# Three attention units take their decay rows from TensorE instead of from DRAM, and the loads of the opening are put in another order

## The chip, the cores and the metric

The kernel runs on one core of a Trainium2 chip. The metric is the device time of one execution in microseconds (us). Times are given as a median over runs; one further execution was recorded by the profiler, and every duration below is from that one.

## The reference

`reference()` chains two blocks. The first is an mLSTM over q, k, v of shape batch 4 x heads 8 x 768 steps x 40, with one input gate, one forget gate and 40 output gates per step:

```python
m_new  = np.maximum(f_gate[:, :, t] + m, i_gate[:, :, t])
f_stab = np.exp(f_gate[:, :, t] + m - m_new)
i_stab = np.exp(i_gate[:, :, t] - m_new)
C = f_stab * C + i_stab * (v_t outer k_t)
n = f_stab * n + i_stab * k_t
y[:, :, t] = sigmoid(o_gate_t) * (C @ q_t) / max(|n . q_t|, 1)
```

The second is `silu(x @ w_in) @ w_out` on the 3072 rows of 320 that result (w_in is 320 x 2048, w_out 2048 x 320). The weights reach the kernel as 64-bit words and are decoded on the chip.

## The kernel before, in words

**Units.** The 768 steps are cut into 6 chunks of 128. A chunk of one batch, with its 8 heads, is a *unit*; there are 24, unit n being chunk n // 4 of batch n % 4. Within a chunk the recurrence is written as attention with a decay matrix: `Dm[s, h, t] = exp(LF[h, t] + a[s, h])` where t >= s, and 0 elsewhere. `LF` is the running sum of the stabilised log forget gates of the chunk, `a` (kept transposed as `aT`) holds the input-gate part. A unit loads `raw` (q and k, two DMAs in `load_qk`), `kvo` (k, v, output gate in one tile, `load_kvo`), `D` (the rows of LF, each spread over all 128 partitions, `load_d`) and, from chunk 1 on, `qt` and `lq` (`load_q`). It then computes `decay` (mask on GpSimd at L355, exponentials on ScalarE at L365, and `fd`, the decay over the whole chunk), `misc` (tanh of the output gate at L370), `scores` (q.k products at L394; VectorE makes `vw` at L406 and multiplies the scores into `D` at L413), `values` (products at L433, then x on VectorE), `state` (products `pu` at L462) and `xpose` (transposition of x, rounded into `xh` with its remainder `xl`).

**Gates.** `gates(lo, hi)` works on 32 rows (batch x head) by hi - lo steps on VectorE: a running maximum `m_t`, elementwise steps, the sums `LF`, the input part `i_t`; a TensorE transposition turns `i_t` into `aT`. `LF` is then written to a DRAM tensor `LFd`, and every unit's `D` is read back from there with a broadcast. Before the change this is done for chunk 0 first and later for chunks 1 to 5.

**Steps.** Three units form a step (8 steps): 384 rows go through the MLP in 16 column blocks fc. `mm1(fc)` makes 8 products into the PSUM tile `ph` (L532); ScalarE and VectorE form the activation `g` (step 0) or its two parts `gh`, `gl`; `mm2(fc)` adds the products with the second weights into three `pout` tiles (L572), two fc later. Step 0 uses the unrounded `wo` (one product per row block), later steps the rounded `woh` with its remainder `wol`.

**Weights.** 18 parts are loaded by `wload` into the ring of ten "big" buffers (`wrc`, `wri` for w_in, `wro` for w_out) and decoded by `wmake`: one ScalarE instruction (L184), four VectorE instructions (L185, L186, L189, L195), then for w_in a rounding on ScalarE (L205, L215) and a remainder on VectorE (L206, L216). The decoding runs beside the first units and step 0.

**Order.** SyncE (SP) issues nearly all DMAs, strictly in program order. The five pieces of later units are mixed into the steps' loop by the table SCHED through `piece(i)`, where unit n's first piece also issues all loads of unit n + 2. The order on TensorE, ScalarE, VectorE and GpSimd is set by the tile scheduler when the program is built; the function `gates` stands in a block that fixes VectorE's order by hand.

The loads of the opening stand in the program like this before the change:

```python
wload(1); units[0].load_qk(); gates(0, L)
units[0].load_kvo(); units[0].load_d(); prepare(0)
units[1].load_qk(); units[1].load_d(); units[1].load_kvo(); wload(1)
units[2].load_qk(); units[2].load_d(); units[2].load_kvo()
units[0].scores(); prepare(1); gates(L, S); wload(2)
```

Of the kernel before, what the change touches and what calls it, by code (L numbers as in the profile page):

```python
# [8 lines left out]
F32 = mybir.dt.float32  # L9
# [8 lines left out]
L = 128  # L18
# [5 lines left out]
UPS = 3  # L24
# [20 lines left out]
def mlstm_mlp_kernel(  # L45
# [35 lines left out]
    woh = cp.tile([128, NFC, DM], F32R, name="woh")  # L81
# [3 lines left out]
    wo, wol = {}, {}  # L85
# [3 lines left out]
    f_t, i_t, m_t, LF = (  # L89
        pb.tile([BH, S], F32, tag="big", name=n) for n in ("f_t", "i_t", "m_t", "LF")  # L90
    )
# [7 lines left out]
    nc.sync.dma_start(bm, bmask)  # L99
    nc.gpsimd.memset(one, 1.0)  # L100

    def gates(lo, hi):
# [22 lines left out]
        nc.sync.dma_start(LFd[:, 0:H, lo:hi], LF[:, lo:hi])  # L125
        nc.scalar.dma_start(LFd[:, H, lo:hi], LF[0:B, lo:hi])
# [93 lines left out]
    def split_out(i):  # L220

        full, hi = wo.pop(i), woh[:, 2 * i : 2 * i + 2, :]
# [46 lines left out]
    class Unit:  # L269
# [5 lines left out]
        def load_d(self):  # L275
            n, c, b = self.n, self.c, self.b
            sl = slice(c * L, (c + 1) * L)
            self.Dm = p3.tile([128, H, L], F32, tag="D", name=f"D{n}")
            nc.sync.dma_start(
                self.Dm, LFd[b, 0:H, sl].unsqueeze(0).broadcast_to([128, H, L])  # L280
            )
# [38 lines left out]
        def load(self):  # L320
            self.load_d()
            self.load_qk()
            self.load_kvo()
            self.load_q()

# [21 lines left out]
        def decay(self, hf):  # L347

            b, c = self.b, self.c
            if hf == 0 and c < NC - 1:  # L350
                self.fd = p3.tile([KS, H], F32, tag="fd", name=f"fd{self.n}")
                nc.scalar.activation(self.fd, self.Dm[:KS, :, L - 1], AF.Exp)  # L352
            d = self.Dm[:, hf * HH : (hf + 1) * HH, :]
            r = b * H + hf * HH
            nc.gpsimd.affine_select(  # L355
                out=d,
                in_=d,
                compare_op=ALU.is_ge,
                fill=NEG,
                base=0,  # L360
                pattern=[[0, HH], [1, L]],
                channel_multiplier=-1,
            )
            for h in range(HH):
                nc.scalar.activation(  # L365
                    d[:, h, :], d[:, h, :], AF.Exp, bias=aT[:, c, r + h : r + h + 1]
                )

# [138 lines left out]
    class Step:  # L507
# [48 lines left out]
        def mm2(self, fc):  # L556
# [7 lines left out]
            if j == 0:  # L564
                ops = [(gh, wo[fc // 2][:, fc % 2, :])]
            else:
                hi, lo = woh[:, fc, :], wol[fc // 2][:, fc % 2, :]
                ops = [(gh, hi), (gh, lo), (gl, hi)]
# [48 lines left out]
    def piece(i):  # L617

        n, k = divmod(i, 5)
        u = units[n]  # L620
        if k == 0:
            if n + 2 < NU:
                units[n + 2].load()
            u.scores()
        elif k == 2:
            u.values()
        elif k == 3:
            u.state()
# [17 lines left out]
    wload(1)  # L646
    units[2].load_qk()
# [124 lines left out]
```

## Time and profile before

| | us |
|---|---|
| runs | 515.27, 519.13, 521.06; median 519.13 |
| the profiled execution: its own time | 516.28 |
| its span | 514.5 |
| TensorE (PE) busy | 483.6 (94% of the span) |
| VectorE (DVE) busy | 335.0 (65%) |
| ScalarE (ACT) busy | 267.2 (52%) |
| GpSimd (POOL) busy | 95.6 (19%) |

The profiled execution took 1.8 us more than its span; the rest lies around the program. A share is an average over the whole span: TensorE's 94% is made of a long stretch without gaps and an opening in which it often stands still. The profile's rows give a start, a duration, the engine, the line, the operation with output and inputs, and in brackets the idle time ahead and what ended it. An fp32 product is recorded as two rows, so "x8" at L394 is four products.

### The profile page before, as it was taken

What the parts mean: (1) busy time and instruction counts of PE and PEld (TensorE: products, weight loads), DVE (VectorE), ACT (ScalarE), POOL (GpSimd) and SP (SyncE); (2) the same over time, 40 slices, a digit from 0 to 9 for tenths busy, and PEclk for the clock granted to TensorE, in tenths of its full rate; (3) what the DMA queues carried; (4) which work ended last, traced back from release to release, by engine and by line L of the source; (5) the groups of instructions that cost most, each with busy time, mean ns of one, the idle gap of its engine ahead of it and who ended that gap; (6) DMA issues with size and microseconds to landing.
All of it is one profiled execution on the core that took longest, in us unless ns stands there. A gap on an engine that the chain in (4) does not pass through costs nothing.

```text
span 514.5 us, 8611 instructions
## 1 busy us (share of the span) xinstructions
PE 483.6 (94%) x3098; PEld 463.4 (90%) x3098; DVE 335.0 (65%) x687; ACT 267.2 (52%) x647; POOL 95.6 (19%) x139
## 2 busy tenths in 40 slices
PE   1498899999999999999999999999899999999996
PEld 1397888888899998999899999999899999999996
DVE  6499999953796677667756597546665654444332
ACT  1556767431775467447664557526664433334332
POOL 0211305321233212313221222112210000000000
PEclk9999999999999999999999999999999999999999
DMA  3999996153476437543560367333660000001001
GB/s 100 301 351 242 256 324 199 33 155 108 129 173 172 122 86 215 156 137 109 183 167 33 108 180 203 105 106 102 189 170 31 29 27 14 0 1 40 0 3 38
DMA packets 52525, 65.54 MB, mean 127 GB/s; under 512 B 3195, under 2 KB 40479, under 8 KB 52483
## 3 DMA queue, kind: packets, MB, share of 16 engines
q1 hardware_dynamic: 48963, 60.95, 42.2%
q10 hardware_dynamic: 3520, 4.04, 2.3%
q8 instruction: 24, 0.39, 0.3%
q14 instruction: 18, 0.15, 0.1%
HBM read 60.94 MB, written 4.04 MB: 126 GB/s over the span
## 4 chain that ended last, share of the span: by engine, by line
PE 68%; DMA 16%; ACT 7%; DVE 4%; issue 2%; SPq 1%; POOL 1%; POOLq 0%; ACTq 0%; DVEq 0%
PE ph L532 28%; PE pout L572 28%; DMA D<-LFd 8%; DMA raw<-in_qk_dram 7%; PE po L433 5%; ACT D L365 3%; PE ps L394 3%; PE po L424 2%; ACT st L338 1%; PE pu L462 1%; PE px L495 1%; DMA lq<-LFd 1%; POOL D L355 1%; DMA wrc<-in_w_in_dram 1%; DVE st L340 1%
## 5 line engine op out<-in xcount | busy, mean ns | idle before, releaser
L532 PE MATMUL ph<-xh,wh 128*128 128x384 f32 x384 | 135.8, 354 | 2.4 <-DVE g L540 1.7
L532 PE MATMUL ph<-xl,wh 128*128 128x384 f32 x384 | 130.2, 339 | 0.0
L545 DVE SCALAR_TENSOR_TENSOR th<-th,ph 128x384 f32<-128x384 f32 x112 | 61.4, 549 | 79.5 <-ACT th L536 79.5
L572 PE MATMUL pout<-woh,gh 128*128 128x320 f32 x336 | 106.9, 322 | 2.1 <-ACT gh L550 2.0
L572 PE MATMUL pout<-wol,gh 128*128 128x320 f32 x336 | 102.8, 308 | 0.0
L551 DVE TENSOR_TENSOR gl<-th,gh 128x384 fp32r<-128x384 f32 x112 | 68.7, 614 | 48.9 <-ACT gh L550 46.6
L536 ACT ACTIVATE th<-ph 128x384 f32<-128x384 f32 x128 | 62.1, 485 | 70.3 <-PE ph L532 63.3
L572 PE MATMUL pout<-woh,gl 128*128 128x320 f32 x336 | 97.9, 312 | 0.6 <-DVE gl L551 0.5
L532 PE MATMUL ph<-xh,wl 128*128 128x384 f32 x256 | 86.9, 339 | 0.0
L550 ACT CAST gh<-th 128x384 fp32r<-128x384 f32 x112 | 56.8, 510 | 48.4 <-DVE th L545 47.1
L532 PEld LDWEIGHTS ph<-xh,wh 128*128 128x128 f32 x384 | 72.8, 190 | 4.7 <-DVE g L540 2.0
L532 PEld LDWEIGHTS ph<-xl,wh 128*128 128x128 f32 x384 | 72.7, 189 | 1.0
L365 ACT ACTIVATE D<-D,aT 128x128 f32<-128x128 f32 x192 | 59.7, 390 | 15.2 <-POOL D L355 15.0
L572 PEld LDWEIGHTS pout<-woh,gh 128*128 128x128 f32 x336 | 63.1, 188 | 3.9 <-ACT gh L550 3.0
L572 PEld LDWEIGHTS pout<-wol,gh 128*128 128x128 f32 x336 | 63.3, 188 | 0.0
L572 PEld LDWEIGHTS pout<-woh,gl 128*128 128x128 f32 x336 | 61.2, 188 | 1.4 <-DVE gl L551 1.2
L433 PEld LDWEIGHTS po<-kvo,D 128*128 128x128 f32 x384 | 54.3, 215 | 1.3 <-ACT wti L184 0.8
L433 PE MATMUL po<-kvo,D 128*128 128x41 f32 x384 | 54.7, 297 | 0.4 <-issue 0.4
L340 DVE TENSOR_TENSOR st<-raw,st 40x512 fp32r<-40x512 f32 x64 | 45.0, 703 | 6.7 <-ACT st L338 5.4
L532 PEld LDWEIGHTS ph<-xh,wl 128*128 128x128 f32 x256 | 48.4, 189 | 0.0
L355 POOL TENSOR_SCALAR_AFFINE_SELECT D<-D 128x512 f32<-128x512 f32 x48 | 32.8, 706 | 77.3 <-ACT fd L352 61.5
L338 ACT CAST st<-raw 120x512 fp32r<-120x512 f32 x64 | 35.9, 621 | 16.1 <-DMA raw<-in_qk_dram 16.1
(77 smaller groups left out, 546.3 us busy)
## 6 DMA issues: line engine op xcount, KB each, us to landing
raw<-in_qk_dram SPq DMA_DIRECT2D x32, 480.0 KB
D<-LFd SPq DMA_DIRECT2D x24, 512.0 KB
kvo<-in_kvo_dram SPq DMA_DIRECT2D x24, 484.0 KB
wro<-in_w_out_dram SPq DMA_DIRECT2D x8, 640.0 KB
wri<-in_w_in_dram SPq DMA_DIRECT2D x8, 512.0 KB
out_dram<-ob ACTq DMA_DIRECT2D x24, 160.0 KB
qt<-in_qp_dram SPq DMA_DIRECT2D x20, 180.0 KB
lq<-LFd SPq DMA_DIRECT2D x60, 60.0 KB
```

The source lines that it names most:

```text
L338: nc.scalar.copy(t, raw)
L340: nc.vector.tensor_tensor(out=t[r0 : r0 + D, :], in0=raw[r0 : r0 + D, :], in1=t[r0 : r0 + D, :].bitcast(F32), op=ALU.subtract,)
L355: nc.gpsimd.affine_select(out=d, in_=d, compare_op=ALU.is_ge, fill=NEG, base=0, pattern=[[0, HH], [1, L]], channel_multiplier=-1,)
L365: nc.scalar.activation(d[:, h, :], d[:, h, :], AF.Exp, bias=aT[:, c, r + h : r + h + 1])
L394: nc.tensor.matmul(ps[:, j, :], k_[:, cs], q_[:, cs], start=True, stop=True)
L433: nc.tensor.matmul(po[:, h, :], self.Dm[:, h, :], self.vt[:, h, :], start=first, stop=(h == H - 1))
L532: nc.tensor.matmul(ph, w, x, start=(i == 0), stop=(i == len(ops) - 1))
L536: nc.scalar.activation(th, ph, AF.Tanh, scale=0.5)
L545: nc.vector.scalar_tensor_tensor(out=th, in0=th, scalar=1.0, in1=ph, op0=ALU.add, op1=ALU.mult)
L550: nc.scalar.copy(gh, th)
L551: nc.vector.tensor_tensor(out=gl, in0=th, in1=gh.bitcast(F32), op=ALU.subtract)
L572: nc.tensor.matmul(self.po[t], g[:, ts], w, start=(fc == 0 and i == 0), stop=(last and i == len(ops) - 1),)
```

## The change

- **Decay rows of units 0, 1, 2 by products.** `load_d` of these units allocates `D` and issues no DMA. `decay` makes, per half of the heads, four products of a column of the identity, broadcast to 128 columns, with `LF` of the chunk (32 rows by 128): each spreads one row of LF over 128 partitions of a PSUM tile `pd`. The exponentials read `pd` and write `D`; the mask follows them, with fill 0 in place of -1e30 ahead of them. The `pd` tiles of units 0 and 1 take buffers of `psO` (three), those of unit 2 buffers of `psH` (two). `fd` is no longer made in chunk 0, where nothing reads it.
- **Gates in one tile.** `f_t`, `i_t`, `m_t`, `LF` are slices of one tile `G` in a pool of one buffer whose next tenant is `woh`; four "big" buffers are thereby free from the start. `gates(0, L)` and `gates(L, S)` stand one behind the other at the beginning; `LF` is written to `LFd` once, for all chunks, by `gates_out` from SP's queue.
- **Loads.** The order of the opening is new (below). In the loop, the loads of unit n + 2 are issued with three pieces of unit n: `kvo` and `D` with the first, `raw` with the second, `qt` and `lq` with the fourth.

```diff
+    pg = pool("pg", 1)
+    G = pg.tile([BH, 4, S], F32, tag="g", name="G")
+    f_t, i_t, m_t, LF = (G[:, i, :] for i in range(4))
...
+    def gates_out():
+        nc.sync.dma_start(LFd[:, 0:H, :], LF)
+        nc.sync.dma_start(LFd[:, H, :], LF[0:B, :])
...
-        nc.sync.dma_start(LFd[:, 0:H, lo:hi], LF[:, lo:hi])
-        nc.scalar.dma_start(LFd[:, H, lo:hi], LF[0:B, lo:hi])
...
+            if n < UPS:
+                return
             nc.sync.dma_start(
                 self.Dm, LFd[b, 0:H, sl].unsqueeze(0).broadcast_to([128, H, L])
...
+            if n < UPS:
+                to, tag = (psH, "h") if n == UPS - 1 else (psO, "o")
+                e = to.tile([128, HH, L], F32, tag=tag, name=f"pd{n}_{hf}")
+                for h in range(HH):
+                    nc.tensor.matmul(
+                        e[:, h, :],
+                        ident[:BH, r + h : r + h + 1].broadcast_to([BH, 128]),
+                        LF[:, c * L : (c + 1) * L],
...
             if n + 2 < NU:
-                units[n + 2].load()
+                units[n + 2].load_kvo()
+                units[n + 2].load_d()
             u.scores()
+        elif k == 1:
+            if n + 2 < NU:
+                units[n + 2].load_qk()
...
-    wload(1)
-    units[0].load_qk()
     with tc.manual_schedule(engines={mybir.EngineType.DVE}):
         gates(0, L)
+        gates(L, S)
+    units[0].load_qk()
+    wload(1)
...
     units[2].load_kvo()
+    gates_out()
+    wload(3)
     units[0].scores()
     prepare(1)
-    gates(L, S)
-    wload(2)
```

**SP's queue, the opening.** `LFd` is the DRAM copy of the gate sums, `D` a unit's decay rows, `wrc`, `wri`, `wro` the weight parts. Before:

```order
L97 DMA f_t<-in_fg_dram 32x768
L99 DMA bm<-in_bmask_dram 120x123
L171 DMA wrc_110<-in_w_in_dram 64x1024
L172 DMA wrc_110<-in_w_in_dram 64x1024
L291 DMA raw_113<-in_qk_dram 40x1024 x2
L125 DMA LFd<-LF 4x8x128
L302 DMA kvo_132<-in_kvo_dram 128x968
L279 DMA D_134<-LFd 128x8x128
L291 DMA raw_153<-in_qk_dram 40x1024 x2
L279 DMA D_156<-LFd 128x8x128
L302 DMA kvo_158<-in_kvo_dram 128x968
```

After the change, from `wrc` on (ahead of it stand only `G<-in_fg_dram` and unit 0's two `raw`):

```order
L172 DMA wrc_143<-in_w_in_dram 64x1024
L173 DMA wrc_143<-in_w_in_dram 64x1024
L307 DMA kvo_146<-in_kvo_dram 128x968
L296 DMA raw_170<-in_qk_dram 40x1024 x2
L307 DMA kvo_174<-in_kvo_dram 128x968
L168 DMA wri_176<-in_w_in_dram 128x2x512
L675 DMA bm<-in_bmask_dram 120x123
L296 DMA raw_179<-in_qk_dram 40x1024 x2
L307 DMA kvo_183<-in_kvo_dram 128x968
L102 DMA LFd<-G 4x8x768
L103 DMA LFd<-G 4x768
L168 DMA wro_187<-in_w_out_dram 128x2x640
```

The write of the gate sums, which the loads of kvo and everything later stood behind, has moved behind the loads of all three units; the weights `wro` now stand behind it, and no row reads `D` for the first three units.

**ScalarE and VectorE, units 0 and 1 after the change.** The first fence is ScalarE from the decoding of the first weight part (L185) on; L389 is the tanh of a unit's output gate, L382 the exponentials.

```order
L185 ACT_TABLE_LOAD
L185 ACTIVATE wtc_259<-wrc_143 128x512
L389 ACTIVATE kvo_146<-kvo_146 128x320
L216 CAST wh<-wtc_259 64x512 x2
L389 ACTIVATE kvo_174<-kvo_174 128x320
L382 ACTIVATE D_148<-pd_0_149,aT 128x128 x4
L382 ACTIVATE D_148<-pd_1_159,aT 128x128 x4
```

The second is VectorE up to unit 0's scores (L432); ahead of its first row stand unit 0's `vw` and the five sums L125 of the later chunks. The G rows are gates of chunks 1 to 5, the wti and wto rows weight decoding, `vw_238` is unit 1's.

```order
L128 TENSOR_TENSOR G<-G 32x640
L186 TENSOR_SCALAR wti_345<-wti_345 128x512
L131 TENSOR_TENSOR G<-G 32x640
L187 TENSOR_SCALAR wti_345<-wti_345 128x512
L190 SCALAR_TENSOR_TENSOR wti_345<-wri_176,wti_345 128x512
L140 COPY aT<-pt_132 128x160
L196 SCALAR_TENSOR_TENSOR wti_345<-wri_176,wti_345 128x512
L425 TENSOR_TENSOR vw_238<-kvo_174,D_173 128x328
L207 TENSOR_TENSOR wl<-wti_345,wh 128x2x256
L186 TENSOR_SCALAR wto_391<-wto_391 128x640
L187 TENSOR_SCALAR wto_391<-wto_391 128x640
L432 TENSOR_TENSOR D_148<-ps_0_193,D_148 128x512
```

Before, the gates' rows stood ahead of every row of unit 0, and the two rows of unit 0's scores followed its `vw` directly; now gates of the later chunks, a part of `w_in` and the first half of the first part of `w_out` stand between them.

**TensorE, the first products of the MLP.** Before, unit 3's values (`po_549`) and state (`pu_591`) stand in the first `ph`:

```order
L433 MATMUL po_549<-kvo_397,D_392 128x41 x4
L532 MATMUL ph_0_459<-xh_284,wh 128x384
L462 MATMUL pu_591<-vw_514,kvo_397 120x123 x2
L462 MATMUL pu_591<-vw_514,kvo_397 80x82
L433 MATMUL po_549<-kvo_397,D_392 128x41 x4
L532 MATMUL ph_0_459<-xl_285,wh 128x384
```

After it, the products of `ph_0` and `ph_1` follow unit 2's transposition directly; the last of `ph_1` (of the products of unit 3, `ps_0_501` and `ps_1_502` are the scores) and what comes then:

```order
L551 MATMUL ph_1_527<-xh_292,wl 128x384
L551 MATMUL ph_1_527<-xh_292,wh 128x384
L551 MATMUL ph_1_527<-xl_293,wh 128x384
L413 MATMUL ps_0_501<-raw_402 128x128 x4
L413 MATMUL ps_1_502<-raw_402 128x128 x4
L551 MATMUL ph_2_566<-xh_292,wh 128x384
```

Unit 3's scores (`ps_0_501`, `ps_1_502`), its values and its state, which stood ahead of the MLP's first products or among them, have moved behind `ph_1` and further.

More of the change, by code (lines that the diff above doesn't have):

```diff
@@ L80, in mlstm_mlp_kernel @@
     wl = cp.tile([128, 2, DFF], F32R, name="wl")
-    woh = cp.tile([128, NFC, DM], F32R, name="woh")
     pq = pool("pq", DFF // 256)
-    wo, wol = {}, {}
+    wo, wol, woh = {}, {}, {}
+    pg = pool("pg", 1)
     BH = B * H
-    f_t, i_t, m_t, LF = (
-        pb.tile([BH, S], F32, tag="big", name=n) for n in ("f_t", "i_t", "m_t", "LF")
-    )
+    G = pg.tile([BH, 4, S], F32, tag="g", name="G")
+    f_t, i_t, m_t, LF = (G[:, i, :] for i in range(4))
     one = cp.tile([BH, 1], F32, name="one")
@@ L98, in mlstm_mlp_kernel @@
     nc.scalar.dma_start(i_t, ig)
-    nc.sync.dma_start(bm, bmask)
     nc.gpsimd.memset(one, 1.0)
+    def gates_out():
+        nc.sync.dma_start(LFd[:, 0:H, :], LF)
+        nc.sync.dma_start(LFd[:, H, :], LF[0:B, :])
     def gates(lo, hi):
@@ L220, in split_out @@
     def split_out(i):
-        full, hi = wo.pop(i), woh[:, 2 * i : 2 * i + 2, :]
+        if not woh:
+            woh[0] = pg.tile([128, NFC, DM], F32R, tag="g", name="woh")
+        full, hi = wo.pop(i), woh[0][:, 2 * i : 2 * i + 2, :]
         to, tag = (pq, "wo") if i else (pw, "wt")
@@ L318, in load_q @@
                     )
[L320 to L324, printed above, removed]
         def split(self, hf, which):
@@ L347, in decay, with mask @@
         def decay(self, hf):
-            b, c = self.b, self.c
-            if hf == 0 and c < NC - 1:
-                self.fd = p3.tile([KS, H], F32, tag="fd", name=f"fd{self.n}")
+            n, b, c = self.n, self.b, self.c
+            if hf == 0 and 0 < c < NC - 1:
+                self.fd = p3.tile([KS, H], F32, tag="fd", name=f"fd{n}")
                 nc.scalar.activation(self.fd, self.Dm[:KS, :, L - 1], AF.Exp)
-            d = self.Dm[:, hf * HH : (hf + 1) * HH, :]
+            d = e = self.Dm[:, hf * HH : (hf + 1) * HH, :]
             r = b * H + hf * HH
[L355 to L363, printed above, removed]
+            if n < UPS:
[6 more added lines that the diff above has]
+                        LF[:, c * L : (c + 1) * L],
+                        start=True,
+                        stop=True,
+                    )
+            def mask(fill):
+                nc.gpsimd.affine_select(
+                    out=d,
+                    in_=d,
+                    compare_op=ALU.is_ge,
+                    fill=fill,
+                    base=0,
+                    pattern=[[0, HH], [1, L]],
+                    channel_multiplier=-1,
+                )
+            if n >= UPS:
+                mask(NEG)
             for h in range(HH):
                 nc.scalar.activation(
-                    d[:, h, :], d[:, h, :], AF.Exp, bias=aT[:, c, r + h : r + h + 1]
+                    d[:, h, :], e[:, h, :], AF.Exp, bias=aT[:, c, r + h : r + h + 1]
                 )
+            if n < UPS:
+                mask(0.0)
         def misc(self):
@@ L566, in mm2 @@
             else:
-                hi, lo = woh[:, fc, :], wol[fc // 2][:, fc % 2, :]
+                hi, lo = woh[0][:, fc, :], wol[fc // 2][:, fc % 2, :]
                 ops = [(gh, hi), (gh, lo), (gl, hi)]
@@ L627, in piece @@
         elif k == 3:
+            if n + 2 < NU:
+                units[n + 2].load_q()
             u.state()
@@ L646, in mlstm_mlp_kernel @@
     wload(1)
+    nc.sync.dma_start(bm, bmask)
     units[2].load_qk()
```

## The prediction

> **What bounds the kernel now.** I read the page's head first, then the windows of each stage, then TensorE's rows in the opening.
>
> ```profile
> span 514.5 us, 8611 instructions
> 5.00:10.00 5.00, 0.00 (x0) 0.00 (x0) 4.07 (x10) 1.94 (x2) 0.00 (x0) 1.00 0.27 79
> 15.00:20.00 5.00, 1.13 (x7) 1.03 (x8) 1.41 (x3) 1.56 (x5) 1.21 (x2) 1.00 1.03 277
> 30.00:40.00 10.00, 10.00 (x54) 9.06 (x53) 8.86 (x22) 5.95 (x14) 0.40 (x1) 1.00 1.04 322
> 40.00:50.00 10.00, 8.61 (x39) 6.95 (x40) 10.00 (x27) 6.72 (x17) 1.67 (x2) 1.00 1.03 247
> 80.00:100.00 20.00, 20.00 (x109) 16.69 (x108) 20.00 (x37) 12.85 (x34) 7.60 (x9) 1.00 0.45 133
> 150.00:200.00 50.00, 50.00 (x347) 49.42 (x347) 36.26 (x74) 30.27 (x79) 13.91 (x21) 1.00 0.52 141
> ```
>
> In a window's row stand its length, then the busy time of TensorE, its weight loads, VectorE, ScalarE and GpSimd, then the clock, the share of the DMA engines and GB/s. From 80 us on TensorE hardly stands still (20.00 of 20, 50.00 of 50): loads there are hidden, and the end moves by what the dense stretch's beginning moves. The opening is another matter. At 5 to 10 us the DMA engines are used to 0.27, since SP's queue stands before the write of the gate sums; from 15 us on they are full. The chain of waits shows what TensorE waited for then:
>
> ```profile
> 2.27 4.22 DMA wrc<-in_w_in_dram
> 19.38 8.59 DMA D<-LFd
> ```
>
> The second row is unit 2's decay rows, 8.59 us from issue to landing. So the change attacks something real: a round trip through DRAM, and 3 x 512 KB of reads. TensorE's rows (start, duration, ..., in brackets the idle time ahead) show what the opening is made of:
>
> ```profile
> 11.47 2.08 PE L394 MATMUL ps<-raw 40*128 40x128 f32 x16
> 23.27 2.07 PE L394 MATMUL ps<-raw 40*128 40x128 f32 x8 [1.73 <-DVE D L413]
> 25.27 1.93 PE L433 MATMUL po<-kvo,D 128*128 128x41 f32 x8
> 41.87 1.42 PE L462 MATMUL pu<-vw,kvo 128*120 128x123 f32 x6 [0.21 <-DVE x L447]
> 44.47 0.69 PE L495 MATMUL px<-ident,x 128*128 128x128 f32 x2 [1.18 <-DVE x L450]
> 45.92 3.09 PE L394 MATMUL ps<-raw 40*128 40x128 f32 x16
> 48.94 0.69 PE L495 MATMUL px<-ident,x 128*128 128x128 f32 x2
> 50.89 1.90 PE L433 MATMUL po<-kvo,D 128*128 128x41 f32 x8 [0.43 <-issue]
> 52.59 0.67 PE L532 MATMUL ph<-xh,wh 128*128 128x384 f32 x1
> 53.06 1.29 PE L462 MATMUL pu<-vw,kvo 128*120 128x123 f32 x6
> 55.79 0.67 PE L532 MATMUL ph<-xl,wh 128*128 128x384 f32 x1
> 56.26 0.52 PE L532 MATMUL ph<-xh,wl 128*128 128x384 f32 x1
> 56.58 0.52 PE L532 MATMUL ph<-xh,wh 128*128 128x384 f32 x1
> 58.60 0.33 PE L532 MATMUL ph<-xh,wl 128*128 128x384 f32 x1
> 58.78 0.33 PE L532 MATMUL ph<-xh,wh 128*128 128x384 f32 x1
> 61.46 0.44 PE L532 MATMUL ph<-xh,wh 128*128 128x384 f32 x1 [1.65 <-DVE g L540]
> ```
>
> Three readings. Unit 0's values begin at 25.27, held by its decay. From there to the first MLP products at 55.79 the engine stands still for only 0.21 + 1.18 + 0.43 = 1.8 us: this stretch is work, not waiting. And that work runs at half speed: at 56.26 and 56.58 the products start 0.32 us apart, at 58.60 and 58.78 0.18. The page prints a clock of 1.00 throughout, so the spacing is what to trust.
>
> **The change part by part.** I follow the new program from its start to its first values product.
>
> ```profile
> 6.57 1.28 ACT L184 ACT_TABLE_LOAD   x1 [6.57 <-DMA wrc<-in_w_in_dram]
> 14.07 1.26 ACT L215 CAST wh<-wtc 64x512 fp32r<-64x512 f32 x2 [5.55 <-DVE wtc L195]
> 19.45 2.44 ACT L365 ACTIVATE D<-D,aT 128x128 f32<-128x128 f32 x8 [0.74 <-POOL D L355]
> 22.79 0.47 ACT L370 ACTIVATE kvo<-kvo 128x320 f32<-128x320 f32 x1 [0.78 <-DMA kvo<-in_kvo_dram]
> 18.79 1.22 POOL L355 TENSOR_SCALAR_AFFINE_SELECT D<-D 128x512 f32<-128x512 f32 x2 [17.48 <-ACT fd L352]
> 8.55 0.43 DVE L185 TENSOR_SCALAR wtc<-wtc 128x512 f32<-128x512 f32 x1 [0.93 <-ACT wtc L184]
> 11.09 0.67 DVE L189 SCALAR_TENSOR_TENSOR wtc<-wrc,wtc 128x512 uint32<-128x512 uint32 x1
> 11.69 1.67 DVE L122 TENSOR_TENSOR_SCAN LF<-one,f_t 32x128 f32<-32x128 f32 x5
> 13.97 0.81 DVE L130 TENSOR_TENSOR i_t<-i_t,LF 32x640 f32<-32x640 f32 x1
> 14.92 0.71 PE L136 MATMUL pt<-ident,i_t 32*128 32x32 f32 x5 [1.37 <-DVE i_t L130]
> 14.20 1.94 SPq L302 DMA_DIRECT2D kvo<-in_kvo_dram  x1
> 22.05 0.63 SPq L125 DMA_DIRECT2D LFd<-LF  x1
> ```
>
> *The products.* 24 of them are added. The trace has none of this kind; the nearest rows are scores products with 40 rows, 0.52 us each where they stand alone (four in 2.07, at 23.27) and 0.26 where two share the time (eight in 2.08, at 11.47). The new ones all use the same 32 rows, so 0.52: 12.4 us, from about 5.5 (the gates begin at 3.6) to about 18. At the lower price they would end near 12. Neither end costs anything: the exponentials that read the last of them stand behind 20 others on ScalarE and come at 19 or later, and TensorE had nothing else to do then. If that cover went, the price is what sticks out, at most 1 us.
>
> *ScalarE's order.* It loads its table only when `wrc` has landed, at 6.57 before. Unit 0's `raw`, 320 KB, now goes ahead of it and `bm`, 58 KB, behind: 262 KB, 0.9 us at 277 GB/s, 2.2 at the 121 GB/s that the row of 4.22 us gives for 512 KB. I take 1.3: 7.9. Table 1.28 and the first decoding 0.66: 9.8. VectorE's four decoding rows, two of each kind, 2.2: 12.0. The two casts 1.26: 13.3. Unit 1's tanh 0.47: 13.8. Only then eight exponentials, 2.44: 16.2, and the second mask, half of 1.22: 16.8. That tanh waits for unit 1's kvo, up to which the queue holds 2.3 MB; at 277 GB/s, from 2.3 us on, it lands near 11. It costs nothing up to 13.3, and one for one from there.
>
> *VectorE's order.* `vw` 0.5: 17.3. The five sums 1.67: 19.0, and LF is whole. Two gate rows of 0.81 and a decoding row of 0.43: 21.0. Transpositions 0.71, then unit 0's scores 2.08 and the first half of unit 1's 2.04: 25.8 on TensorE. Meanwhile SP writes the sums (two issues, 1.4) and issues the first `wro` at 20.4. In an all but empty queue 512 KB took 4.22, so 4.3: 24.7. Two ScalarE and VectorE steps on it, 0.8 and 1.0, stand ahead of unit 0's scores: 26.4. The row itself 0.65 frees the bank for the other half of unit 1's scores, 2.05. **Unit 0's values begin at 29.1, 3.8 us later than at 25.27.** The wait for D has become a wait for the weights.
>
> *From there to the MLP.* Before, 25.27 to 55.79 is 30.5 us. Out of it go the 1.8 of idle time, unit 3's scores (45.92 to 48.94: 3.0) and its values and state with one product of `ph` (50.89 to 55.79: 4.9), which now stand behind `ph_1`. That leaves 20.8: `ph_0` begins at 49.9 and not at 55.8.
>
> *What was put off.* It comes back at full speed:
>
> ```profile
> 92.96 1.08 PE ps L394 x8
> ```
>
> Eight records, four products, in 1.08: unit 3's scores 2.2. For its values and state I halve the 4.4 of before: 2.2. The sixteen products of `ph_0` and `ph_1` take 4.0 of 55.79 to 59.8 for fifteen, so 4.3. The change of speed came 2.5 us after the dense products began; they now begin at another moment, and every further microsecond at half speed costs about 0.45, so 0 to 1.5, taken as 0.8. The idle 1.65 ahead of 61.46 goes, since unit 3's scores now lie there; if VectorE is late all the same, it stays. Sum: 49.9 + 4.3 + 0.8 + 2.2 + 2.2 = 59.4, against 61.46 for the same work: **2.1 us earlier**, 0.4 if the gap stays. Behind this point the loop's new load order matters only if TensorE waits there. The longest row of its waits from 62 us on is
>
> ```profile
> PE pout L572 <- ACT gh L550: 2.0, 3, 1.2
> ```
>
> 2.0 us in three waits, none of the list for a DMA. I count nothing, plus or minus 1 us; the cover is TensorE's own work, and a load that came late would cost one for one.
>
> The profiled execution took 516.28, which gives 514.2. It lies near the fast end of the runs; their median of 519.13 gives 517.0. Part of that spread may be the opening's transfers, which half leave the path, so I set 516.
>
> **A rule against the trace.** In the window of 30 to 40 us TensorE is busy 10.00 of 10 and yet at half speed. The Trainium skill ("TensorE: Matmul & The Clock Gate", "Part 1: The HAM clock gate") says that the clock doubles after one busy window of some 3.4 us. By that rule the 12 us of new products would lift it at once, and the idle time behind them, from 18 to 21, is too short for it to fall: that is the first rival, and its 510 to 511. The trace disagrees as far as records show busy time: they filled 10 us without a rise. Products with few rows or columns may not count as busy; no run here shows it.
>
> **The rivals.**
>
> *The engine goes fast early.* The new products are a longer unbroken run than any ahead of 29.98 before. If they lift the clock and it holds, the 20.8 us to the MLP shrink towards 11. VectorE then binds: it is full in 40 to 50 (10.00 of 10) and would hold `ph_0` near 46, 4 us earlier than in the sum; with 1 to 2 us in `ph_0` and `ph_1` that is 5 to 6 more, 510 to 511. Against it: the long run at 30 to 40 lifted nothing, and the scores at 45.92, 40 rows like the new products' 32, neither.
>
> *VectorE holds step 0.* It is full from 40 to 100 (20.00 of 20 in 80 to 100) with weight decoding, which the change leaves as it is. If TensorE overtakes it, the gain is eaten and the time is 518 to 519. For it: that full stretch, and the 1.65 us wait. Against it: only that one wait.
>
> *The weights come late (slower).* Unit 0's scores stand behind `wro` on VectorE, and `wro` behind the gate sums on SP. In the full queue unit 1's kvo took from 14.20 to 22.79, 8.6 us. Had `wro` that, everything from 25.8 on would move 4.3 later: 521 or so, and with unit 1's tanh held as long, 524. It decides from a landing at 26.8 on, where the 2.1 are gone. For it: three engines wait in a row there. Against it: the queue should be empty by 18.
>
> That the round trip stays is ruled out for units 0 to 2: SP's rows have no read of D for them.
>
> **How the numbers follow.** Forecast 0.50 (513 to 519); fast early 0.18 (508 to 513); VectorE 0.15 (518 to 520); late weights 0.17 (520 to 525). A measurement here tells about 1%, 5.2 us: under 514 faster, over 524.3 slower. Faster: the second case and a third of the first, 0.35. Slower: half of the fourth and a little, 0.10. The rest, 0.55, is within. The range 508 to 523 leaves out the two far ends.
>
> **What would show it.** Right: no D rows before unit 3's; values from 28 to 30; `ph_0` at 49 to 51, spacing 0.32 and then 0.18 within 6 us; no `g` wait ahead of `ph_2`. Wrong: 0.18 spacing or scores of 0.27 each before 45; `wro` landing after 27; TensorE waiting for `wh` or `wo` in 60 to 100; or new waits behind 110, where the loop's load order would show.

## The result, and the profile after

The changed kernel takes 514.4 us (median of 20 runs, 508.8 to 518.4) beside 516.7 for the kernel before in the same session: a ratio of 0.9937, 95% interval 0.9908 to 0.9965. A repetition gave 514.4 beside 515.6, ratio 0.9969, with an interval (0.9932 to 1.0006) that touches 1. Medians are over all runs, ratios over the fast runs alone (runs more than 1.5% above a kernel's fastest are left out), so a ratio can differ a little from the quotient of the medians. The size of the forecast, 516.0 and 2 to 3 us less than before, was right. Its origin, as the experiments show, was not.

The profiled execution of the changed kernel took 516.9 us. It contains 10.2 us at half clock behind 138 and 213 us, which the execution shown of before does not have, so only its opening is compared directly.

The page's head and the windows (columns as in the prediction) of the changed kernel:

```profile
span 515.2 us, 8685 instructions
5.00:10.00 5.00, 4.38 (x20) 4.41 (x21) 0.87 (x3) 1.75 (x2) 0.00 (x0) 1.00 1.03 266
15.00:20.00 5.00, 2.07 (x8) 1.77 (x8) 4.90 (x7) 5.00 (x20) 3.17 (x4) 1.00 0.21 70
30.00:40.00 10.00, 10.00 (x54) 9.40 (x54) 10.00 (x23) 3.33 (x5) 1.02 (x1) 1.00 0.59 206
100.00:150.00 50.00, 47.81 (x283) 42.40 (x282) 35.08 (x67) 22.08 (x55) 14.20 (x19) 0.93 0.45 125
```

The DMA engines now work from 5 us on (1.03 where it was 0.27) and have little to do from 15 to 20 (0.21 where it was 1.03), since the three reads of decay rows are gone and the other loads that ran then before now come earlier. From 5 to 10 TensorE has the new products. The last row shows the half clock as a mean of 0.93 over the window.

TensorE's rows in the opening of the changed kernel (start, duration, engine, line, operation, count, idle time ahead in brackets):

```profile
5.62 4.60 PE L360 MATMUL pd<-G,ident 32*128 32x128 f32 x20 [5.62 <-DVE G L125]
10.09 4.61 PE L360 MATMUL pd<-G,ident 32*128 32x128 f32 x20
15.43 2.07 PE L360 MATMUL pd<-G,ident 32*128 32x128 f32 x8 [0.73 <-ACT D L382]
23.82 0.74 PE L137 MATMUL pt<-ident,G 32*128 32x32 f32 x5 [6.31 <-DVE G L131]
24.49 3.78 PE L413 MATMUL ps<-raw 40*128 40x128 f32 x24
28.90 2.07 PE L413 MATMUL ps<-raw 40*128 40x128 f32 x8 [0.63 <-DVE D L432]
30.90 1.93 PE L452 MATMUL po<-kvo,D 128*128 128x41 f32 x8
51.86 0.69 PE L551 MATMUL ph<-xh,wh 128*128 128x384 f32 x1 [0.57 <-ACT xh L521]
55.82 0.49 PE L551 MATMUL ph<-xh,wh 128*128 128x384 f32 x1
56.14 0.35 PE L551 MATMUL ph<-xl,wh 128*128 128x384 f32 x1
56.95 1.71 PE L413 MATMUL ps<-raw 40*128 40x128 f32 x16
58.59 0.44 PE L551 MATMUL ph<-xh,wh 128*128 128x384 f32 x1
```

The 48 records of the 24 products end at 17.5, and 6.31 us of idle time follow. Unit 0's values begin at 30.90, 5.6 us later than before, and the first MLP product stands at 51.86, 3.9 us earlier than the 55.79 at which before's dense products began. Products are 0.32 us apart up to 56.14 and 0.18 to 0.19 from there. Unit 3's scores stand behind the two product groups, 1.71 us where they cost 3.09 before. Nothing waits ahead of `ph_2`. Its start at 58.59 and unit 3's values and state, 2.30 (61.72 to 64.02), make 60.9 for the work that before had behind it at 61.46: 0.6 us gained, not 2.1.

Why the values are later than forecast stands on VectorE and GpSimd in the same stretch:

```profile
15.45 0.63 POOL L369 TENSOR_SCALAR_AFFINE_SELECT D<-D 128x512 f32<-128x512 f32 x1 [14.07 <-ACT D L382]
20.48 2.28 POOL L369 TENSOR_SCALAR_AFFINE_SELECT D<-D 128x512 f32<-128x512 f32 x2 [0.54 <-ACT D L382]
15.58 1.17 DVE L114 TENSOR_TENSOR G<-G 32x640 f32<-32x640 f32 x1
16.79 1.14 DVE L117 TENSOR_TENSOR G<-G 32x640 f32<-32x640 f32 x1
19.10 2.05 DVE L125 TENSOR_TENSOR_SCAN G<-one,G 32x128 f32<-32x128 f32 x5
21.08 1.18 DVE L128 TENSOR_TENSOR G<-G 32x640 f32<-32x640 f32 x1
22.19 0.84 DVE L186 TENSOR_SCALAR wti<-wti 128x512 f32<-128x512 f32 x1
```

Gate rows of 32x640 took 1.14 to 1.18 beside the masks and 0.81 in the trace of before; the five sums 2.05 for 1.67; a decoding row 0.84 for 0.43. The decay masks of the first units, which now follow the exponentials, fall upon VectorE's gate rows. In the chain, the two transfers of the sum came nearly as forecast:

```profile
2.59 5.57 DMA wrc<-in_w_in_dram
22.44 3.93 DMA wro<-in_w_out_dram
```

### The profile page after: what moved, and what is told of

Same layout as the page of the kernel before. It is cut to its first block, busy times and chain, and to the rows that moved or that the text cites. A ratio compares the mean times of both kernels' runs of the same rounds, so it can differ in the third digit from the quotient of the medians.

```text
span 515.2 us, 8685 instructions
## 1 busy us (share of the span) xinstructions
PE 493.1 (96%) x3146; PEld 475.1 (92%) x3146; DVE 339.5 (66%) x687; ACT 266.7 (52%) x643; POOL 101.0 (20%) x139
## 4 chain that ended last, share of the span: by engine, by line
PE 76%; DMA 11%; DVE 6%; ACT 4%; issue 1%; SPq 1%; POOL 0%; POOLq 0%; ACTq 0%
PE ph L551 30%; PE pout L591 28%; PE po L452 8%; DMA D<-LFd 7%; PE ps L413 3%; PE pu L481 3%; DMA raw<-in_qk_dram 2%; PE po L443 2%; PE px L514 1%; ACT D L382 1%; DMA wrc<-in_w_in_dram 1%; DVE st L339 1%; ACT st L337 1%; DMA out_dram<-ob 1%; DMA wro<-in_w_out_dram 1%
## 5 line engine op out<-in xcount | busy, mean ns | idle before, releaser
L564 DVE SCALAR_TENSOR_TENSOR th<-th,ph 128x384 f32<-128x384 f32 x112 | 61.2, 549 | 77.5 <-ACT th L555 77.0
L591 PE MATMUL pout<-woh,gh 128*128 128x320 f32 x336 | 109.2, 327 | 1.1 <-ACT ob L608 0.7
L591 PE MATMUL pout<-wol,gh 128*128 128x320 f32 x336 | 104.0, 311 | 0.0
L591 PE MATMUL pout<-woh,gl 128*128 128x320 f32 x336 | 100.1, 313 | 0.5 <-DVE gl L570 0.5
L569 ACT CAST gh<-th 128x384 fp32r<-128x384 f32 x112 | 56.9, 510 | 51.6 <-DVE th L564 48.3
L369 POOL TENSOR_SCALAR_AFFINE_SELECT D<-D 128x512 f32<-128x512 f32 x48 | 36.3, 776 | 124.5 <-ACT fd L351 66.0
L382 ACT ACTIVATE D<-D,aT 128x128 f32<-128x128 f32 x168 | 53.6, 391 | 9.6 <-POOL D L369 9.6
L339 DVE TENSOR_TENSOR st<-raw,st 40x512 fp32r<-40x512 f32 x64 | 46.9, 734 | 10.9 <-ACT st L337 9.3
L392 POOL TENSOR_TENSOR qt<-qt,lq 120x384 f32<-120x384 f32 x20 | 24.6, 1232 | 84.2 <-ACT lq L391 84.2
```

The lines of the kernel that those rows point to most:

```text
L339: nc.vector.tensor_tensor(out=t[r0 : r0 + D, :], in0=raw[r0 : r0 + D, :], in1=t[r0 : r0 + D, :].bitcast(F32), op=ALU.subtract,)
L369: nc.gpsimd.affine_select(out=d, in_=d, compare_op=ALU.is_ge, fill=fill, base=0, pattern=[[0, HH], [1, L]], channel_multiplier=-1,)
L382: nc.scalar.activation(d[:, h, :], e[:, h, :], AF.Exp, bias=aT[:, c, r + h : r + h + 1])
L392: nc.gpsimd.tensor_tensor(out=self.qt, in0=self.qt, in1=self.lq, op=ALU.mult)
L564: nc.vector.scalar_tensor_tensor(out=th, in0=th, scalar=1.0, in1=ph, op0=ALU.add, op1=ALU.mult)
L569: nc.scalar.copy(gh, th)
```

## The experiments

All times are medians of device time. Ratios are to the kernel before, measured beside each, with 95% intervals.

### 1. The changed kernel with the old loop

```diff
         if k == 0:
             if n + 2 < NU:
-                units[n + 2].load_kvo()
                 units[n + 2].load_d()
+                units[n + 2].load_qk()
+                units[n + 2].load_kvo()
+                units[n + 2].load_q()
             u.scores()
-        elif k == 1:
-            if n + 2 < NU:
-                units[n + 2].load_qk()
         elif k == 2:
             u.values()
         elif k == 3:
-            if n + 2 < NU:
-                units[n + 2].load_q()
             u.state()
```

> The changed kernel with the loop's loads as they were before: all loads of unit n + 2 with the first piece of unit n. Theory (the opening decides, the loop's load order counts for nothing): the time of the changed kernel, 514.4, within 1.5 us; the opening's rows unchanged, unit 0's values at 30.9. Rival (the new places of the loads are what gains): back to 516.7 or above. Second rival (the new places cost something, since TensorE waits and a half-speed clock stand at 116 to 145 us in the changed kernel's profile): 511 to 513, and no such waits.

**520.4 us, ratio 1.0055 (1.0027 to 1.0083).** With the loop's loads put back the changed kernel is slower than before, 6 us behind itself: the first rival. The opening is the same (first MLP product at 52.3). What differs lies behind it. ScalarE and TensorE of this run at 91 to 97 us:

```profile
93.84 0.47 ACT L389 ACTIVATE kvo<-kvo 128x320 f32<-128x320 f32 x1 [1.87 <-DMA kvo<-in_kvo_dram]
94.22 0.47 ACT L555 ACTIVATE th<-ph 128x384 f32<-128x384 f32 x1
96.51 0.56 PE L551 MATMUL ph<-xh,wh 128*128 128x384 f32 x1 [2.96 <-DVE g L559]
96.87 0.52 PE L551 MATMUL ph<-xl,wh 128*128 128x384 f32 x1
```

Unit 6's raw waits on SP for a big buffer (issued at 87.0), its kvo stands behind it (88.15), the tanh of kvo waits until 93.84, the activation `th` of the MLP stands behind that on ScalarE, and TensorE waits 2.96 us for `g`. Then its products go at 0.32 us apart again until 100 (the trace's clock record has half speed from 96.7 to 100.1). The rule by which I counted the loop at nothing, that TensorE has no wait for a DMA there, looked at the wrong queue: the wait comes in through ScalarE's order.

### 2. Before with the decay products alone

```diff
         def load_d(self):
...
+            if n < UPS:
+                return
...
+            if n < UPS:
...
+                for h in range(HH):
+                    nc.tensor.matmul(
+                        e[:, h, :],
+                        ident[:BH, r + h : r + h + 1].broadcast_to([BH, 128]),
+                        LF[:, c * L : (c + 1) * L],
...
+            if n >= UPS:
+                mask(NEG)
...
+            if n < UPS:
+                mask(0.0)
```

> The kernel before with the decay products alone: no reads of D for units 0 to 2, the gates, the loads and their order as before. Theory (what is gained is the round trip of D, what is lost is the place of the gates and of the first output weights): unit 0's values well ahead of both 25.3 and 30.9, at 21 to 24, and the time below the changed kernel's, 510 to 513. Rival (removing the round trip is worth nothing since VectorE's weight decoding or the later loads bind): 516 to 517, like before.

**521.9 us, ratio 1.0110 (1.0077 to 1.0144): slower, which neither theory had.** The last products end at 29.5 and not at 17.5, among the first units' scores and values. The first MLP product stands at 55.5, the next at 57.5, and the clock rises at 62.0. `ph_2` then begins at 62.26, only 0.8 us later than before's 61.46; what the opening doesn't show, two stretches at half clock behind 89 and 209 us (3.4 us each) do in part.

### 3. The changed kernel with the second gates free

```diff
     with tc.manual_schedule(engines={mybir.EngineType.DVE}):
         gates(0, L)
-        gates(L, S)
+    gates(L, S)
```

> The changed kernel with the gates of chunks 1 to 5 outside the block that fixes VectorE's order, so that their rows need not wait behind the copy of aT of chunk 0, but fill VectorE's idle time from 6.0 to 10.2 us. Theory (unit 0's values are held by VectorE's gate rows: LF whole at 21.1, slowed by GpSimd's masks beside them): LF whole at 12 to 14, the first output weights landing at 18 to 20, unit 0's values at 23 to 26, the time 4 us below the changed kernel, 509 to 512. Rival (the stretch to the MLP is held by VectorE's weight decoding anyway): values earlier but the first ph at 51 to 52 still, 513 to 515.

**518.9 us, ratio 1.0036 (1.0006 to 1.0067): slower than either theory.** The values begin at 26.58, 4.3 us earlier, and the time is 4 us longer:

```profile
26.58 3.63 PE L452 MATMUL po<-kvo,D 128*128 128x41 f32 x16
55.49 0.67 PE L551 MATMUL ph<-xh,wh 128*128 128x384 f32 x1
57.52 0.67 PE L551 MATMUL ph<-xl,wh 128*128 128x384 f32 x1
```

The scheduler puts unit 3's scores, values and state ahead of `ph_0` again, all at half speed, and the dense products begin at 57.5. So earlier weights alone gain nothing; what stands ahead of `ph_0` counts.

### 4. Filler products in the idle time of the opening

```diff
+FILLERS = 5
...
+    fill = psO.tile([128, HH, L], F32, tag="o", name="fill")
+    for r in range(FILLERS):
+        nc.tensor.matmul(
+            fill, ident, ident.unsqueeze(1).broadcast_to([128, HH, L]), start=True, stop=True
+        )
```

> The changed kernel with five fp32 products of 128 rows by 512 columns of the identity with itself, which nobody reads, in TensorE's idle time of 6.3 us ahead of the transpositions at 23.8. Theory (full-height products lift the clock, and half speed holds the stretch from 24 to 52): the fillers start 1.7 us apart and then 0.85; unit 0's scores at 0.13 each in pairs and not 0.26; the first ph 3 to 6 us earlier and its products 0.18 apart from the start; 508 to 511 unless the clock falls again in the values. Rival (the clock does not rise, or falls at once): 514 to 516, with the transpositions 1 to 3 us later.

**518.9 us, ratio 1.0036 (1.0004 to 1.0068): slower than either theory.** It answers the question of the clock:

```profile
17.42 5.97 PE L686 MATMUL fill<-ident 128*128 128x512 f32 x10
24.24 1.16 PE L414 MATMUL ps<-raw 40*128 40x128 f32 x16
29.73 3.74 PE L414 MATMUL ps<-raw 40*128 40x128 f32 x16 [4.32 <-DVE aT L141]
```

After the fillers sixteen records of scores take 1.16 us, where the changed kernel needed 3.78 for 24: full speed at 24 us. The trace's clock record has it rise at 20.3, 2.9 us after the first filler, and fall at 27.1. The second sixteen take 3.74. The fillers moved the copy of `aT` back in VectorE's order, which is the wait of 4.32 us, and the first MLP product comes at 54.39, 2.5 us later than in the changed kernel. Thus products of 128 rows by 512 columns lift the clock; the change's own products, 9 us without a pause at 5.62 but with 32 rows by 128 columns, did not.

### 5. Before with the new loop alone

```diff
             if n + 2 < NU:
-                units[n + 2].load()
+                units[n + 2].load_kvo()
+                units[n + 2].load_d()
             u.scores()
+        elif k == 1:
+            if n + 2 < NU:
+                units[n + 2].load_qk()
...
         elif k == 3:
+            if n + 2 < NU:
+                units[n + 2].load_q()
             u.state()
```

> The kernel before with nothing but the loop's new load order (unit n+2's kvo and decay rows with the scores of unit n, its raw one piece later, its q two later). Theory A (the order is worth something only where a raw load meets a buffer that comes free late, as in the changed kernel with the old loop, and before's raw wait ended at 79 us without a gap on TensorE): 515.5 to 518, no shorter gaps behind 62 us than before's 4.8 us in sum. Theory B (the order is good in itself, whatever the opening): 511 to 513.5, gaps behind 62 us under 2 us.

**512.5 us, ratio 0.9940 (0.9906 to 0.9974): all of the change's gain, without products and without early gates.** The time is Theory B's. Its gaps behind 62 us are 3.9 in sum, not under 2, but 3.1 of these are one wait for `g` ahead of 90.76, in step 0; what changed lies behind it. The sum rows of the six windows from 100 to 400 us, in the same columns as above, first of before, then of this kernel:

```profile
sum 300.00, PE 294.90 PEld 285.55 DVE 197.59 ACT 166.99 POOL 71.48; mean PE 49.15 PEld 47.59 DVE 32.93 ACT 27.83 POOL 11.91
```

```profile
sum 300.00, PE 299.25 PEld 292.44 DVE 206.36 ACT 168.44 POOL 78.00; mean PE 49.87 PEld 48.74 DVE 34.39 ACT 28.07 POOL 13.00
```

TensorE stands still for 5.1 us of these 300 before and for 0.75 with the new loop. The largest part of the cause shows in what ScalarE waits for, before and then here (total us, times, longest):

```profile
ACT st L338 <- DMA raw<-in_qk_dram: 16.1, 8, 3.2
```

```profile
ACT st L338 <- DMA raw<-in_qk_dram: 2.6, 3, 1.3
```

In experiment 1, with the old loop and the new opening, this wait is 15.9 in 9; in the changed kernel 3.1 in 4. It follows the loop and not the opening. Before has nine gaps of 0.15 us and more on TensorE in this stretch, 4.85 us in sum. Five of them, 3.2 us, end a chain that begins with such a wait of the casts for raw. Two (0.7 us) stand behind a wait of ScalarE for decay rows and one (0.7 us) behind a wait for `lq`; these waits became shorter too with the new loop (25.3 to 12.6 us and 17.9 to 13.2 in sum).

### 6. The changed kernel once more

> The changed kernel once more, for a second profile and time. Theory A (the stretches at half clock follow from small gaps that the program's own order makes): the same gaps of 0.3 to 1 us near 135 to 138 and 212 us, 513 to 516 in time, half-clock stretches there again or, where a gap is shorter, none. Theory B (the half-clock stretches come from outside the core): gaps as before, stretches at other places. First MLP product at 51.4 to 52.4 in both.

**514.4 us, ratio 0.9969 (0.9932 to 1.0006).** First MLP product at 53.2; the profiled execution was its slowest, 523.3 us. The gaps at 136.0, 137.4 and 138.5 (0.16, 0.34 and 0.85 us) are those of the first profile, and half clock follows from 139.9 to 146.7 again; another stretch follows a gap of 1.69 at 174.5, and none came behind 213. So the stretches come after gaps (theory A), and part of the gaps recurs. In the first profile of the changed kernel:

```profile
135.13 0.41 PE L591 MATMUL pout<-woh,gh 128*128 128x320 f32 x1 [0.43 <-ACT gh L569]
138.37 3.64 PE L452 MATMUL po<-kvo,D 128*128 128x41 f32 x16 [0.86 <-DVE D L432]
141.81 0.61 PE L591 MATMUL pout<-woh,gh 128*128 128x320 f32 x1
```

and, in its chain for that place,

```profile
124.51 8.30 DMA D<-LFd
```

A unit's decay rows, asked for at 124.51, took 8.3 us; ScalarE stood still for 3.73 us ahead of `fd`, which reads them, with its casts of raw behind it, so VectorE's share of those casts and its `D` came late in turn. The sixteen values records then take 3.64 us, the half-speed price of the opening.

### 7. Free gates, and the MLP ahead of unit 3 by a written order

```diff
+    first = tc.manual_schedule(engines={mybir.EngineType.PE})
+    first.__enter__()
     for j in range(NSTEP):
...
-            while done < min(want, 5 * NU):
+            while done < min(want, 5 * NU) and (j or fc):
...
+            if j == 0 and fc == 2:
+                first.__exit__(None, None, None)
```

on top of experiment 3.

> The changed kernel with the second stretch of gate rows free to be ordered with VectorE's other work (as in the third experiment), and with TensorE's order written out over the first three pieces of the MLP, so that unit 3's scores, values and state stand behind ph_1. Theory A (the two gains, earlier weights and unit 3 put off, add up): values at 26.6, first MLP product 20.9 later at 47.5, 509.5 to 512. Theory B (VectorE, full from 40 us on, holds the first pieces): the first product at 49 or later or gaps of 2 us and more in ph_0 to ph_2, 514 to 517.

**512.5 us, ratio 0.9927 (0.9891 to 0.9963).** The time lies between the theories, just above A; the first MLP product is where B has it:

```profile
26.28 3.63 PE L452 MATMUL po<-kvo,D 128*128 128x41 f32 x16
49.56 0.66 PE L514 MATMUL px<-ident,x 128*128 128x128 f32 x2 [1.74 <-DVE Cm L503]
51.62 0.69 PE L551 MATMUL ph<-xh,wh 128*128 128x384 f32 x1 [0.57 <-ACT xh L521]
```

The values begin 4.6 us ahead of the changed kernel, the first MLP product 0.2. But VectorE is not what holds most of it: it is busy for only 7.13 of the 10 us from 40 to 50 and itself waits 2.38 for a `po` there. Of the 4.4 us lost between values and MLP, 1.74 are the wait for VectorE, 1.15 are four records of identity products that now lie between unit 0's values and its state (until 31.1), and 1.0 is that unit 2's scores take 3.09 and not 2.08.

### 8. Before with the new loop, and the MLP ahead of unit 3

The order of experiment 7, without the products and the early gates.

> The kernel before with the loop's new load order, and with TensorE's order written out so that unit 3's scores, values and state stand behind ph_1: no identity products, gates as before. Theory A (what the change gained is that unit 3's work was put off past the change of speed): values at 25.3, first MLP product near 48, same work done at 57 to 58 instead of 61.5, 512 to 514. Theory B (VectorE sets the pace of the first pieces, so the order of TensorE's work counts for nothing): gaps of 2 us and more in ph_0 to ph_2, 516 to 518.

**511.6 us, ratio 0.9935 (0.9900 to 0.9970).** Against experiment 5 (0.9940) putting unit 3 off is worth nothing that can be told. TensorE now waits 4.0 us in two waits for `x`, and then 1.83 for `g` at 60.6; in the clock record full speed begins at 57.8, is lost from 61.2 to 71.5 and costs about half of these 10.2 us. In the trace Theory B is nearer, since waits for VectorE hold the first pieces, though the one gap within them is just under 2 us; the time is below A's range, by the loop.

### 9. Before with the order of four calls changed

```diff
-                units[n + 2].load()
+                units[n + 2].load_kvo()
+                units[n + 2].load_d()
+                units[n + 2].load_qk()
+                units[n + 2].load_q()
```

> The kernel before with the order of the loop's loads changed, but all of them still issued with the first piece of unit n: kvo, decay rows, raw, q of unit n+2. Theory A (the gain of the new loop is that kvo and the decay rows no longer stand behind raw's wait for its buffer): 511.5 to 513.5, as with the whole new loop (512.5). Theory B (the gain is that raw is asked for a piece later, when less stands ahead of it in the DMA engines, so that ScalarE's casts of it seldom wait: 16.1 us in 8 waits before, 2.6 in 3 with the whole new loop): 515 to 518, with 10 us or more of such waits left.

**510.2 us (6 runs), ratio 0.9894 (0.9856 to 0.9931): the lowest median of all, below both theories, though its interval overlaps that of experiment 5.** `load()` gives D, raw, kvo, q; moving kvo to the head of that group is worth 1.1%. ScalarE's rows at the same place of the two kernels show how. Before:

```profile
296.56 1.13 ACT L338 CAST st<-raw 120x512 fp32r<-120x512 f32 x2
300.63 1.14 ACT L338 CAST st<-raw 120x512 fp32r<-120x512 f32 x2 [2.94 <-DMA raw<-in_qk_dram]
301.68 0.48 ACT L536 ACTIVATE th<-ph 128x384 f32<-128x384 f32 x1
302.06 0.50 ACT L550 CAST gh<-th 128x384 fp32r<-128x384 f32 x1
```

and TensorE, then:

```profile
302.61 0.41 PE L572 MATMUL pout<-woh,gh 128*128 128x320 f32 x1 [0.68 <-ACT gh L550]
```

Experiment 9:

```profile
296.64 1.15 ACT L338 CAST st<-raw 120x512 fp32r<-120x512 f32 x2
297.69 2.45 ACT L365 ACTIVATE D<-D,aT 128x128 f32<-128x128 f32 x8
300.04 1.12 ACT L338 CAST st<-raw 120x512 fp32r<-120x512 f32 x2
```

The last two casts of raw come within 0.6 us of each other in both, since raw waits for its buffer either way (33.7 us of such waits on SP in sum here, 57.9 before). But here eight decay exponentials stand between the casts in ScalarE's order, and before ScalarE stood still with the MLP's `th` and `gh` behind the casts, until TensorE waited. The unit's values and state come later with its exponentials: on TensorE they now stand from 302.4 to 303.8, at the place where TensorE of before waited for `gh`. All the casts' waits are 2.0 us in 2, and TensorE's idle time from 100 to 400 us is 0.33 where it was 5.1. That is 4.8 us, beside 5.3 between the medians; the two profiled executions are only 3.2 apart, since this one, its slowest run, has longer waits ahead of 100 us and 3.4 us at half clock from 93.6. Theory A named the order rightly and put it down to kvo's wait; in fact ScalarE waits longer for kvo than before (25.5 us to 6.9), at places where nothing urgent stands behind.

### 10. Products and new loop, gates as before

Experiment 2 with the loop of experiment 5.

> The kernel before with the identity products (and the masks behind the exponentials) and with the new loop, but with the gates, the small loads and the home of the second weights as before. With the old loop the products cost 5.2 us (521.9 against 516.7). Theory A (that was the old loop's raw load, met at a bad moment, so it goes with the new loop): 511 to 514. Theory B (the products themselves hold the opening up, the clock rising near 62 us in place of 58): 515.5 to 518.5.

**524.0 us, ratio 1.0133 (1.0083 to 1.0184).** Theory B, and more than it said:

```profile
10.79 5.46 PE L363 MATMUL pd<-LF,ident 32*128 32x128 f32 x24 [10.79 <-DVE LF L122]
19.75 3.76 PE L363 MATMUL pd<-LF,ident 32*128 32x128 f32 x16
57.33 0.67 PE L554 MATMUL ph<-xh,wh 128*128 128x384 f32 x1
63.86 0.44 PE L554 MATMUL ph<-xh,wh 128*128 128x384 f32 x1
```

Against experiment 5 the first MLP product is 5.8 us later (57.3 to 51.5), the clock rises 5 us later, and `ph_2` begins 3.8 us later (63.86 to 60.05): so much of the delay lasts. 10.2 us at half clock behind 93 and 148, where experiment 5 has 3.4, take an estimated 3.4 more, and TensorE's waits behind 62 us are 8.0 in sum where they were 3.9. That makes 11.3 of the 12.4 us between the two profiled spans (11.5 between the medians), and only a third of it lies in the opening; why the waits behind it grew was not followed. In the changed kernel the same products lie in idle time, with the early gates and the new order of the small loads.

### 11. Unit 3 still later

Experiment 7 with unit 3's pieces behind `ph_2`: `(j or fc)` becomes `(j or fc > 1)`.

> As the experiment with free gates and TensorE's written order (512.5 us), but with unit 3's pieces one product group later still, behind ph_2, so that VectorE makes g of ph_0 ahead of unit 3's work. Theory A (unit 3's work on VectorE is what holds the first pieces): first MLP product at 50 or earlier, 509.5 to 511.5. Theory B (VectorE is full with decoding weights from 30 us on whatever the order, so the first product stays at 51 to 52): 512 to 514.

**512.6 us, ratio 0.9956 (0.9924 to 0.9988).** Theory B: first MLP product at 51.65, again 1.74 ahead of the last `px`. The clock rises at 54.9, 2.3 us earlier than in experiment 7, though the first products come at the same time; the median does not follow.

### 12. The changed opening with the loop of experiment 9

```diff
                 units[n + 2].load_kvo()
                 units[n + 2].load_d()
+                units[n + 2].load_qk()
+                units[n + 2].load_q()
             u.scores()
-        elif k == 1:
-            if n + 2 < NU:
-                units[n + 2].load_qk()
         elif k == 2:
             u.values()
         elif k == 3:
-            if n + 2 < NU:
-                units[n + 2].load_q()
             u.state()
```

> The changed kernel's opening with the loop of the ninth experiment (kvo, decay rows, raw and q of unit n+2 all with the first piece of unit n, in that order). Theory A (the opening of the change, products and early gates together, is worth nothing or costs up to 4 us once the loop's order is right: 512.5 with the old opening and the new loop against 514.4 with both, 510.2 with the old opening and this loop): 512 to 515. Theory B (the opening gains the 2.1 us of the prediction, and what separated 514.4 from 512.5 was spread between runs): 507.5 to 509.5.

**514.0 us, ratio 0.9945 (0.9912 to 0.9979).** Theory A: with the loop in order, the new opening gains nothing on the old (0.9894). Its profiled execution was its best, 508.45 with a span of 506.7, no stretch at half clock behind 56 us, and the opening of the changed kernel (first MLP product at 52.0). The best run of experiment 9 is 509.05. So at their best the openings are alike; why this one has more runs above 514 was not settled.

The two by two, as ratios to before: old opening and old loop 1; new loop alone 0.9940; new opening alone 1.0055; both 0.9937 and 0.9969. The loop is worth 0.6% with the old opening and 0.9 to 1.2% with the new. The opening costs 0.55% with the old loop and 0 to 0.3% with the new, where the intervals overlap; with the loop of experiment 9 it is 0.5% (0.9894 to 0.9945), and they overlap again.

## Why the prediction was right in size and wrong in its reason

The size came out by luck: the opening, which was to bring 2.1 us, brought nothing that the medians show, and the loop, which was to bring nothing, brought the gain.

- **Products hidden at no cost.** Right for this kernel: they ended at 17.5 (18 forecast), 0.46 us each (0.52). The cover I named, that TensorE had nothing else to do, came with the early gates and the order of the small loads; without them (experiment 10) the products cost 11.5 us, 3.8 of them in the opening. I had put the price without cover at 1 us at most. That bound was wrong, since it left out that products stand between other work at half speed.
- **ScalarE's order.** Right within 0.6 us: `wrc` until 8.24 (7.9), unit 1's tanh done at 14.35 (13.8).
- **VectorE's order: the term that was mis-sized.** LF was whole at 21.1, not 19.0. I had `vw` wait for ScalarE's exponentials and a mask; the chain instead runs through VectorE's own rows, which leave no hole from 12.5 to 21.1. Of the 2.1 us, 1.4 are rows that ran longer beside GpSimd's masks than their like before (1.17 and 1.14 for 0.81, one of 0.81 for 0.47, the sums 2.05 for 1.67); the other 0.7 is the length of this chain, which I had not summed. Two rows behind the sums add 0.8. The Trainium skill ("SBUF — State Buffer", "Who interferes with whom") says that the port pair which VectorE and GpSimd share goes as a lock to one of them for a whole instruction; these rows agree, at 0.3 to 0.4 us each, and my sum took durations from rows that had no mask beside them.
- **`wro` and the values.** The first `wro` was issued at 22.44 and landed at 26.4: 3.93 us for a forecast of 4.3, moved by the 2.1 above. Values at 30.90 for 29.1.
- **From there to the MLP 20.8 us.** 20.96 measured. `ph_0`, `ph_1` and the clock's change 5.1; measured 51.86 to 56.95, 5.1. Unit 3's scores 1.7 for 2.2, values and state 2.3 for 2.2; no wait for `g`. The opening's gain, 2.1 forecast, is 0.6 in the profile, and the medians show no gain.
- **The loop's loads at 0, plus or minus 1: the step that failed.** They are worth 3.1 us with the old opening (0.6% of 515.6) and 4 to 6 with the new, which is the whole gain. I judged them by the list of what TensorE waits for, saw no DMA in it, and called them covered. The trace of before had the answer in the wait of 16.1 us of ScalarE's casts for raw, which stand two instructions ahead of the `gh` for which TensorE waited.
- **The engine goes fast early.** It did not. The new products ran for 9 us and changed nothing, so the trace disagrees with the rule of the Trainium skill ("TensorE: Matmul & The Clock Gate", "Part 1: The HAM clock gate") as far as records are taken for activity. The fillers agree with it (a rise after 2.9 us). So not every product counted here: those with 128 rows and 512 columns did, those with 32 rows and 128 columns didn't.
- **VectorE holds step 0.** Not the bound in the changed kernel. In experiments 7 and 11 the values come 4.6 us earlier and the MLP at 51.6 all the same, but only 1.74 us of that is a wait for VectorE.
- **Late weights.** The landing at 26.4 was just short of the 26.8 from which I had it decide.

## What to carry to other kernels

When loads of a loop are put in another order, don't ask whether the busiest engine waits for a DMA. Ask for each load which in-order engine meets it first, and what stands behind that instruction: here a wait of ScalarE for raw held the MLP's activation. And where a change has several parts, price them apart, by two by two at least: this one's visible half (products, early gates) gave nothing, and the order of the loads in the loop gave all.

## What the runs showed of the hardware

- **When the clock falls.** A trace's clock record is made of stretches at full and at half speed. Behind the first rise all of them except the last, which the kernel's end cuts off, are whole multiples of 3.41 us long (24, 2, 20, 1 and 87 of them in the changed kernel's first profile). Cut on that grid, the fourteen traces agree: each of the fifteen falls to half clock ahead of 500 us comes at the end of a 3.41 us interval in which TensorE was busy for 0.13 to 0.71 of the time. Eleven more intervals at full clock with 0.50 to 0.71 brought none, and no interval with more than 0.71 brought one. So what bears on the clock is how busy a whole interval is and not the length of one gap; up to 0.71 it went either way. A small gap can be enough: 0.99 us ahead of 212.97 in the changed kernel brought 3.4 us at half clock, while 1.65 us ahead of 61.46 before brought nothing. The Trainium skill ("TensorE: Matmul & The Clock Gate", "Part 1: The HAM clock gate") has the half clock come back after an idle window of some 3.4 us; here intervals of that length that were busy for up to 0.71 were enough, and the measurement decides.
- **What it costs.** Each 3.4 us at half clock costs an estimated 1.7, half of it. In the changed kernel's first profile 1.64 us of gaps at 135 to 138 brought 6.8 us at half clock: the pauses cost less than what followed.
- **What lifts it.** Products with 32 rows and 128 columns did not lift the clock in 9 us (5.62 to 14.7); products of 128 rows with 512 columns did in 2.9 (17.42 to 20.3). Height alone is not enough: from 35.4 to 41.6 us the kernel before ran nothing but products of 128 rows, with 41 to 128 columns, and the clock rose at 58.3. Whether 32 rows with 512 columns would do, no run shows. The same grid sets the moment: experiments 7 and 11 begin their MLP at 51.62 and 51.65, with intervals that begin at 50.4 and 51.5, and the clock rises at 57.2 and 54.9.
